# A hand-ordered attention and two-layer kernel: its order of steps rewritten, the last output bank cut into three pieces, all last stores issued from SyncE

## The chip, the cores and the metric

The kernel runs on one core of a Trainium2 chip. The metric is the time of one execution in device microseconds (us). Before the change it is 221.39 us, the median of three runs (221.13 to 222.2).

## The reference

There are 8 batches with 8 heads, 512 tokens and 32 states per head, and 64 numbers per vector. Per batch and head, attention runs both ways between tokens `x` and states `state`; per token the heads' results are put side by side, and the 8 x 544 rows of 512 go through two layers with a PReLU between them.

```python
scores  = scale * x @ state.T;  a  = softmax(scores);   xread = a  @ state   # 512 token rows
scores2 = scale * state @ x.T;  a2 = softmax(scores2);  sread = a2 @ x       # 32 state rows
x = concat([xread, sread]) -> rows of 512                                    # 4352 x 512
h = x @ w_in                                                                 # 512 -> 2048
g = max(h, 0) + alpha * min(h, 0)
out = g @ w_out                                                              # 2048 -> 512
```

## The kernel before

**The order is written out by hand.** `ORDER` (lines 17 to 101) is a list of some 1,050 tokens. Each names a step and its arguments (table `steps`, line 585), and the loop at line 599 issues them one after another. Nothing else orders the work: each engine runs its own instructions in the order of the tokens and waits for data and free buffers. So a token that is moved is moved past others only on the engines and queues that it uses. Batches are called groups below: 0 to 7 are the token rows of the batches, group 8 stands for the state rows of all batches.

**What the tokens are.** In `S.2.3.6` the numbers are the group, the block of 128 token rows and the pair of inner blocks; a further number is the PSUM bank (0 to 5), which is named when a tile is opened. A letter a, v or p says whether ScalarE, VectorE or GpSimd does a step.

- *Loads, all from GpSimd's queue:* `lx0.g` (half of the first group's x, line 177), `lst` (states, 190), `wi.f` (a quarter of w_in, 196), `wo.i` (a quarter of w_out, 202), `lx.b` (x of group b, 161; buffer of 4). `id` builds the identity for transposes on GpSimd, between loads.
- *Transposes:* `xt`/`xo` turn x of groups 0 and 1 on TensorE and copy it out (276, 281); `xd.b` does it by DMA from SyncE's queue for the later groups (268). `stc`, `stt`, `sto`, `str`, `sro` do the states (236, 230, 244, 258). `Z` issues products of zeros (215).
- *Scores:* `sc.b` (290; `sc.0.0` and `sc.0.1` are halves of group 0) writes the tile "two", which spans two banks. For the token direction follow `sb` (VectorE transposes 32x32 blocks, 323), `smax` (331), `ssh` (subtract, 337), `sexp` (343), `ssum` (347, 348), `snorm` (351) and `wb` (transpose back, 359). For the state direction `tm` (371), `te` (382), `tsum` (392), `tn` (GpSimd multiplies by 1/sum, 396), `tt` (DMA transpose from SyncE's queue, 400), `rd` (state reads on TensorE, 415) and `rdo` (copy out, 426).
- *The first layer is folded into the states:* `m.b.f` multiplies the states of group b with a quarter f of w_in (440, products of 64*32), in two halves: into two banks when banks are named, otherwise into tile "two". `mo` casts each half to SBUF (462).
- *First layer:* `F.b.jc` multiplies those by the attention weights (473; for group 8 it is w_in by the state reads, 482); `f` is one half of it (494). `N` makes relu(-h) on ScalarE (505) and `G` the PReLU on VectorE (513).
- *Second layer:* `S.b.q.j` adds two of 16 products into one bank (525); `R` is the same for group 8 (570). `O` and `RO` copy a finished bank to SBUF and store it from SyncE's queue (562, 563, 580, 582).
- *The last bank* (group 7, block 3) is cut in two halves of 256 columns, in banks of their own: `L.7.3.i` (542) and `LO.7.3.i` (553, 554). A store by `LO` goes out from ScalarE's queue if ScalarE made the copy, else from SyncE's.

A bank is taken again only when its last reader is done: a product that opens a bank can wait for a copy on ScalarE or VectorE, and all products behind it on TensorE wait too.

Of the kernel before, what the change touches and what calls it, by code (L numbers as in the profile page):

```python
# [8 lines left out]
F32 = mybir.dt.float32  # L9
# [8 lines left out]
lx0.0 stc id lx0.1 Z.1.22 stt.0 lst Z.2.20 xt.0.0.0.1 xo.0.0.0.a sto.v xt.0.1.0.2 oma xo.0.1.0.v  # L18
Z.0.4 xt.0.0.1.3 sc.0.0 sb.0.0 smax.0.0 xt.0.1.1.4 xo.0.0.1.a xo.0.1.1.a Z.0.3 str.1.5 sc.0.1 wi.0
lx.1 str.0.0 wi.1 ssh.p.0.0 sb.0.1 smax.0.1 Z.1.3 sc.0 sro.1.a Z.5.7 m.0.0.1.2 sro.0.a ssh.p.0.1  # L20
sexp.0.0 mo.0.0.a.1 tm.0 m.3.0.3.4 sexp.0.1 ssum.0.0 mo.0.0.a.0 mo.3.0.a.0 wo.0 snorm.p.0.0 te.0.0
ssum.0.1 snorm.p.0.1 m.1.0.5.0 Z.2.8 m.2.0.2.1 xt.1.0.0.3 mo.2.0.a.0 xt.1.1.1.2 mo.1.0.a.0 wi.2 wo.1
mo.1.0.v.1 wb.0.0 xt.1.0.1.0 xo.1.0.0.v wb.0.1 xt.1.1.0.5 xo.1.1.1.v mo.3.0.a.1 te.0.1 f.0.0.0.3
mo.2.0.a.1 xo.1.0.1.v f.0.0.1 tsum.0 N.0.0 xo.1.1.0.v m.1.1.4.2 m.0.1 mo.0.1.v.0 f.0.1.0.0
mo.0.1.a.1 f.0.1.1 wi.3 F.0.3.1 tn.0.1 F.0.7.5 mo.1.1.v.0 N.0.1 f.0.2.0.4 mo.1.1.a.1 f.0.2.1 F.0.5.2
wo.2 G.0.0 N.0.3 G.0.1 N.0.2 N.0.7 tn.0.0 G.0.3 N.0.5 lx.2 G.0.2 m.4.0 F.0.4.3 mo.4.0.a.1 S.0.0.0.0
G.0.7 S.0.1.0.1 S.0.0.1 S.0.1.1 N.0.4 m.0.2.4.5 G.0.5 mo.4.0.a.0 sc.1 S.0.2.0.2 G.0.4 mo.0.2.a.0
m.1.2.3.4 wo.3 mo.0.2.a.1 mo.1.2.a.1 S.0.2.1 F.0.6.5 mo.1.2.a.0 sb.1 tm.1 N.0.6 F.0.9.4 F.0.10.3
S.0.0.2 S.0.2.2 G.0.6 N.0.9 smax.1 te.1.1 S.0.1.2 te.1.0 F.0.11.5 N.0.11 S.0.1.3 S.0.2.3 G.0.9 m.0.3
# [5 lines left out]
S.0.0.7 O.0.0.a tm.2 F.1.5.2 lx.3 S.0.3.6 G.1.3 N.1.5 F.1.9.1 G.1.5 tn.1.0 xd.3 te.2.0 F.1.1.0 N.1.1
F.1.4.4 S.0.3.7 te.2.1 F.1.7.2 G.1.6 rd.0.3 N.1.4 O.0.3.a m.2.3 G.1.1 tt.1 F.1.8.0 F.1.10.5 smax.2
rdo.0.a mo.2.3.a.0 S.1.1.0.3 S.1.1.1 N.1.7 G.1.4 N.1.9 S.1.1.2 F.1.11.4 N.1.10 G.1.7 S.1.2.0.2
S.1.1.3 G.1.9 S.1.2.1 ssh.p.2 F.1.13.1 G.1.10 F.1.12.5 N.1.8 G.1.8 N.1.11 sexp.2 N.1.13 S.1.1.4
N.1.12 F.1.15.0 G.1.11 ssum.2 S.1.2.2 G.1.12 N.1.15 F.1.14.4 S.1.2.3 S.1.1.5 N.1.14 S.1.2.4 S.1.2.5
mo.2.3.a.1 G.1.13 G.1.15 m.2.1.5.1 m.3.2 S.1.2.6 G.1.14 snorm.p.2 mo.3.2.v.1 S.1.1.6 mo.3.2.a.0  # L40
# [12 lines left out]
S.2.3.4 S.2.3.5 S.2.3.6 G.3.4 m.4.1.3.2 G.3.14 te.4.1 m.4.3.1.0 ssh.p.4 m.5.1 sexp.4 G.3.2
mo.4.1.v.1 mo.4.1.v.0 mo.4.3.a.0 mo.4.3.v.1 ssum.4 rd.3.5 rd.2.2 F.3.0.1 mo.5.1.a.1 S.2.2.0.3
rdo.2.a F.3.11.0 lx.6 snorm.p.4 N.3.0 F.3.3.2 mo.5.1.a.0 S.2.2.1 N.3.11 S.2.2.2 G.3.0 S.2.2.3
S.2.3.7 F.3.10.1 G.3.11 N.3.3 G.3.3 rdo.3.a wb.4 m.4.2.5.0 tsum.4 mo.4.2.a.1 sc.5 F.3.5.2 S.2.2.4
S.2.2.5 tm.5 F.4.2.0 S.2.2.6 mo.4.2.a.0 N.3.10 tn.4.0 N.3.5 S.3.1.0.5 G.3.5 S.2.2.7 S.3.1.1 F.4.7.2
N.4.2 O.2.3.a tn.4.1 te.5.0 S.3.0.0.4 G.3.10 O.2.2.a N.4.7 G.4.2 F.3.12.1 G.4.7 F.4.6.0 S.3.1.2
# [46 lines left out]
def kernel(  # L105
# [526 lines left out]
```

## Time and profile before

| | |
|---|---|
| median of 3 runs | 221.39 us |
| profiled execution | 221.47 us |
| its span, first to last instruction | 219.7 us |
| TensorE products | 210.4 us busy, 1667 instructions |
| VectorE / ScalarE / GpSimd | 166.0 / 137.3 / 71.1 us busy |
| DMA moved | 23.12 MB, 8.62 of them from GpSimd's queue |
| granted TensorE clock | 1.000 of full speed |

All times in the profile count from the first instruction of the span. A row of the timeline gives the start, how long the group of instructions lasted, the engine (PE is TensorE's products, PEld its weight loads, DVE VectorE, ACT ScalarE, POOL GpSimd, SP SyncE), the line, the operation, output and input tiles, the shape, the count, and in brackets how long the engine had been idle and who ended that. Products overlap: one starts while the one before still drains, so the difference of two starts tells what a group costs. A row of a group of instructions gives the busy total, the mean of one in ns, and the idle time before them. A row of the DMA issues gives the KB of each and the us from issue to landing.

### The profile page before, as it was taken

What the parts mean: (1) busy time and instruction counts of PE and PEld (TensorE: products, weight loads), DVE (VectorE), ACT (ScalarE), POOL (GpSimd) and SP (SyncE); (2) the same over time, 40 slices, a digit from 0 to 9 for tenths busy, and PEclk for the clock granted to TensorE, in tenths of its full rate; (3) what the DMA queues carried; (4) which work ended last, traced back from release to release, by engine and by line L of the source; (5) the groups of instructions that cost most, each with busy time, mean ns of one, the idle gap of its engine ahead of it and who ended that gap; (6) DMA issues with size and microseconds to landing.
All of it is one profiled execution on the core that took longest, in us unless ns stands there. A gap on an engine that the chain in (4) does not pass through costs nothing.

```text
span 219.7 us, 4233 instructions
## 1 busy us (share of the span) xinstructions
PE 210.4 (96%) x1667; PEld 102.0 (46%) x1667; DVE 166.0 (76%) x251; ACT 137.3 (63%) x269; POOL 71.1 (32%) x58
## 2 busy tenths in 40 slices
PE   8678999999999999999999999999999999999992
PEld 7442334444344444544444444444446555644451
DVE  1499989899899989998867998598778775762022
ACT  2598974698699756977573987573665474631010
POOL 7289333452323493371713254003530000000000
PEclk9999999999999999999999999999999999999999
DMA  7999999998891176758930217110132011101034
GB/s 71 184 196 182 187 201 159 157 151 171 100 221 48 51 95 160 149 82 152 230 98 0 95 48 177 52 64 0 48 97 98 0 48 52 48 0 48 3 143 143
DMA packets 41028, 23.12 MB, mean 105 GB/s; under 512 B 24112, under 2 KB 36784, under 8 KB 41008
## 3 DMA queue, kind: packets, MB, share of 16 engines
q0 software_dynamic: 12704, 8.62, 28.2%
q1 hardware_dynamic: 26096, 14.09, 25.5%
q10 hardware_dynamic: 2208, 0.14, 0.7%
q8 instruction: 13, 0.21, 0.4%
q14 instruction: 7, 0.06, 0.1%
HBM read 17.31 MB, written 8.91 MB: 119 GB/s over the span
## 4 chain that ended last, share of the span: by engine, by line
PE 83%; DMA 8%; ACT 2%; POOL 2%; DVE 2%; issue 1%; POOLq 0%; ACTq 0%
PE o L525 45%; PE h L473 24%; DMA w_in_sb<-in_moe_w_in_dram 5%; PE m_ps L440 3%; PE h L482 3%; PE o L570 3%; DMA xT<-xg 3%; PE sr_ps L415 2%; PE o L542 2%; ACT neg L505 1%; DVE m L462 1%; ACT m L462 1%; POOL xg L177 1%; PE sc L290 1%; DVE gt L513 1%
## 5 line engine op out<-in xcount | busy, mean ns | idle before, releaser
L525 PE MATMUL o<-w_out_sb,gt 128*128 128x512 f16 x496 | 124.4, 379 | 0.1
L505 ACT ACTIVATE neg<-h 128x512 f32<-128x512 f32 (+1 forms) x144 | 78.6, 583 | 45.6 <-PE h L473 34.9
L513 DVE SCALAR_TENSOR_TENSOR gt<-neg,oma_sb,h 128x512 f16<-128x512 f32 x128 | 89.5, 738 | 15.0 <-ACT neg L505 14.3
L525 PEld LDWEIGHTS <-gt 128*128 128x128 f16 x496 | 47.8, 98 | 56.5 <-issue 2.1
L473 PE MATMUL h<-aT,m 128*128 128x512 f16 x250 | 69.6, 380 | 0.5 <-ACT m L462 0.4
L473 PEld LDWEIGHTS <-m 128*128 128x128 f16 x250 | 23.6, 98 | 29.9 <-issue 3.5
L462 ACT CAST m<-m_ps 128x512 f16<-128x512 f32 x49 | 28.0, 603 | 7.9 <-PE m_ps L440 4.0
L396 POOL TENSOR_SCALAR e<-e,r 128x512 f16<-128x512 f16 x16 | 25.0, 1566 | 19.3 <-DVE r L392 13.4
L337 POOL TENSOR_TENSOR ts<-ts,mx 128x1024 f32<-128x1024 f32 (+1 forms) x9 | 15.5, 1718 | 45.8 <-DVE mx L331 45.8
L351 POOL TENSOR_TENSOR an<-ts,r 128x1024 f16<-128x1024 f32 (+1 forms) x9 | 15.4, 1718 | 22.6 <-DVE r L348 14.1
L562 ACT COPY osb<-o 128x512 f32<-128x512 f32 x22 | 12.7, 591 | 12.3 <-PE o L525 12.3
L562 DVE COPY osb<-o 128x512 f32<-128x512 f32 x9 | 6.2, 687 | 14.7 <-PE o L525 14.7
L382 ACT ACTIVATE e<-sc,nb 128x512 f16<-128x512 f32 x16 | 11.0, 698 | 1.7 <-DVE nb L374 1.7
L440 PE MATMUL m_ps<-w_in_sb,stT 64*32 64x512 f16 x256 | 11.7, 383 | 0.2 <-DMA w_in_sb<-in_moe_w_in_dram 0.2
L513 DVE SCALAR_TENSOR_TENSOR gs<-neg,oma_sb,h 128x256 f16<-128x256 f32 x16 | 7.3, 478 | 5.6 <-ACT neg L505 5.6
L462 DVE CAST m<-m_ps 128x512 f16<-128x512 f32 x15 | 9.7, 677 | 1.2 <-PE m_ps L440 1.0
L347 DVE TENSOR_REDUCE r<-ts 128x32 f32<-128x1024 f32 (+1 forms) x9 | 9.8, 1090 | 1.0 <-ACT ts L343 0.9
L359 DVE STREAM_TRANSPOSE aT<-an 128x1024 f16<-128x1024 f16 (+1 forms) x9 | 10.1, 1120 | 0.5 <-POOL an L351 0.5
L331 DVE TENSOR_REDUCE mx<-ts 128x32 f32<-128x1024 f32 (+1 forms) x9 | 9.8, 1091 | 0.1
L371 DVE TENSOR_REDUCE nb<-sc 128x2 f32<-128x1024 f32 x8 | 9.6, 1198 | 0.0
L323 DVE STREAM_TRANSPOSE ts<-sc 128x1024 f32<-128x1024 f32 x7 | 8.7, 1240 | 0.6 <-PE sc L290 0.6
L570 PE MATMUL o<-w_out_sb,gs 128*128 128x512 f16 x32 | 9.0, 379 | 0.0
(48 smaller groups left out, 116.7 us busy)
## 6 DMA issues: line engine op xcount, KB each, us to landing
out_dram<-osb SPq DMA_DIRECT2D x31, 256.0 KB, 2.3
xg<-in_x_dram POOLq DMA_DIRECT2D x7, 512.0 KB, 7.3
w_in_sb<-in_moe_w_in_dram POOLq DMA_DIRECT2D x4, 512.0 KB, 9.6
w_out_sb<-in_moe_w_out_dram POOLq DMA_DIRECT2D x4, 512.0 KB, 10.7
xg<-in_x_dram POOLq DMA_DIRECT2D x2, 256.0 KB, 4.9
out_dram<-osr SPq DMA_DIRECT2D x2, 256.0 KB, 2.5
st<-in_state_dram POOLq DMA_DIRECT2D x1, 224.0 KB, 5.8
e2T<-e SPq DMA_TRANSPOSE x8, 3.4
```

What stands on the lines that cost most here:

```text
L337: engine(e).tensor_tensor(ts, ts, over_blocks(cols(live["mx", b], j, S // N)), ALU.subtract)
L351: engine(e).tensor_tensor(blocks(cols(live["an", b], j, S)), blocks(cols(live["ts", b], j, S)), over_blocks(cols(live["r1", b], j, S // N) ...
L382: nc.scalar.activation(live["e2", b][:, g, :, :], live["sc", b][:, :, :, g, :].rearrange("p r j s -> p (r j) s"), EXP, bias=live["nb", b][ ...
L396: nc.gpsimd.tensor_scalar_mul(e2, e2, live["r2", b][:, g : g + 1])
L440: nc.tensor.matmul(t[N * k : N * (k + 1), :], st_head(b, h)[64 * r : 64 * r + 64, :], w_in_sb[64 * r : 64 * r + 64, c, 512 * f : 512 * (f ...
L462: copier(e)(m_tile(b)[:, f, g, :], live["mp", b, f][g])
L473: nc.tensor.matmul(h.rearrange("p (r j s) -> p r j s", r=2, j=2), ms[b][:, f, g, 128 * j : 128 * (j + 1)], weights(b, g), start=(g == 0), ...
L505: nc.scalar.activation(neg, h, RELU, bias=0.0, scale=-1.0)
L513: nc.vector.scalar_tensor_tensor(gt, negs.pop((b, jc)), oma_sb[:, jc : jc + 1], h, ALU.mult, ALU.add)
L525: nc.tensor.matmul(outs[b, q], gts[b, jc][:, 128 * q : 128 * (q + 1)], w_out_sb[:, jc, :], start=(jc == 0), stop=(jc == n_jc - 1),)
L562: copier(e)(osb, t)
L570: nc.tensor.matmul(outs[B, q], gts[B, jc][:, 128 * q : 128 * (q + 1)], w_out_sb[:, jc, :], start=(jc == 0), stop=(jc == n_jc - 1),)
```

## The change

1. `ORDER` is replaced as a whole. The same products are there, with these differences in what is issued: `id` comes after both `lx0`; `sc.0.0` comes ahead of `xt.0.1.1` and `xt.0.0.1`; `m.0.1` and others get banks of their own or tile "two"; small products (`m`, `sc`, `rd`) are gathered into fewer stretches, one of them of eight; `tt.0` stands ahead of `xd.2`, and `rd.0` right behind `sc.2`; `lx.4` stands ahead of `lx.3`; `ssh.5`, `snorm.5` and `snorm.7` go from GpSimd to VectorE; several copies change between ScalarE and VectorE; 64 products of zeros instead of 67.
2. The last bank is cut into pieces of 256, 128 and 128 columns instead of two of 256.
3. All stores of `LO` are issued from SyncE.
4. The outputs of group 2 (`O.2.q`) are stored as two halves of 256 columns each.

```diff
 ORDER = """
-lx0.0 stc id lx0.1 Z.1.22 stt.0 lst Z.2.20 xt.0.0.0.1 xo.0.0.0.a sto.v xt.0.1.0.2 oma xo.0.1.0.v
-Z.0.4 xt.0.0.1.3 sc.0.0 sb.0.0 smax.0.0 xt.0.1.1.4 xo.0.0.1.a xo.0.1.1.a Z.0.3 str.1.5 sc.0.1 wi.0
...
-F.0.8.4 G.0.11 mo.0.3.v.0 S.0.0.3 S.0.3.0.5 N.0.10 ssh.p.1 xd.2 mo.0.3.a.1 S.0.3.1 N.0.8 sexp.1
...
-S.1.2.7 mo.2.1.a.1 mo.2.1.a.0 S.1.1.7 O.1.2.a O.1.1.a m.3.1.0.4 sc.3 m.2.2.1.5 lx.4 S.1.0.0.2 wb.2
...
-L.7.3.1.3 L.7.3.1.4 L.7.3.0.5 O.7.0.a L.7.3.0.6 L.7.3.1.5 O.6.3.a O.7.1.v L.7.3.1.6 RO.0.v L.7.3.0.7
-LO.7.3.0.v L.7.3.1.7 LO.7.3.1.a
+stc lx0.0 lx0.1 oma id Z.1.20 stt.0 Z.2.18 xt.0.0.0.1 sto.a xt.0.1.0.2 xo.0.0.0.v lst xo.0.1.0.v
+Z.0.6 sc.0.0 xt.0.1.1.3 xt.0.0.1.4 sb.0.0 xo.0.0.1.v smax.0.0 xo.0.1.1.a str.0.5 sc.0.1 str.1.0 wi.0
...
+F.0.13.0 sexp.1 tn.0.1 S.0.2.4 N.0.13 S.0.3.3 ssum.1 G.0.13 S.0.0.4 F.0.14.3 tn.0.0 S.0.2.5 tt.0
+S.0.1.4 N.0.14 G.0.14 F.0.12.0 m.1.3 S.0.3.4 snorm.p.1 F.0.15.3 xd.2 S.0.3.5 wb.1 N.0.12 S.0.1.5
...
+mo.2.1.a.0 m.3.2 S.1.1.3 F.1.10.3 F.1.13.0 mo.2.1.a.1 S.1.1.4 N.1.10 F.1.15.1 ssum.2 G.1.10 S.1.2.3
+N.1.13 N.1.14 N.1.15 S.1.2.4 G.1.13 S.1.1.5 mo.3.2.a.1 G.1.14 S.1.2.5 S.1.2.6 mo.3.2.a.0 sc.3
+m.3.1.3.0 G.1.15 m.2.2.2.1 snorm.p.2 S.1.2.7 wb.2 S.1.1.6 mo.3.1.a.1 mo.3.1.a.0 S.1.1.7 tt.1
...
+O.2.0.a S.2.3.7 G.3.7 O.2.1.v m.6.0 m.5.0.2.4 m.4.2.1.5 G.3.1 O.2.3.a mo.6.0.a.1 rd.2.3 mo.6.0.v.0
+mo.4.2.a.0 rd.3.0 snorm.p.4 mo.5.0.a.1 mo.4.2.v.1 m.4.1.1.5 sc.5 rdo.2.v rdo.3.v lx.6 mo.5.0.a.0
+mo.4.1.a.0 m.5.1.3.4 mo.4.1.a.1 mo.5.1.a.0 F.3.10.0 S.2.2.0.2 F.3.11.1 F.3.5.5 N.3.10 S.2.2.1
...
+LO.7.3.1.v R.1.7 L.7.3.2.1 RO.1.v L.7.3.0.6 L.7.3.0.7 S.7.1.7 L.7.3.2.2 LO.7.3.0.v O.7.1.a L.7.3.2.3
+L.7.3.2.4 L.7.3.2.5 L.7.3.2.6 L.7.3.2.7 LO.7.3.2.a
 """

-    def second_half(b, q, i, jc2, k=None):
-        w = d_model // 2
+    pieces = ((0, 256), (256, 384), (384, 512))
+
+    def second_piece(b, q, i, jc2, k=None):
+        lo, hi = pieces[i]
+        w = hi - lo
...
-                w_out_sb[:, jc, w * i : w * (i + 1)],
+                w_out_sb[:, jc, lo:hi],
...
-    def second_half_out(b, q, i, e):
-        w = d_model // 2
-        osb = moe.tile([128, w], F32, name=f"osb_{b}_{q}_{i}", tag="osr", bufs=2)
+    def second_piece_out(b, q, i, e):
+        lo, hi = pieces[i]
+        osb = moe.tile([128, hi - lo], F32, name=f"osb_{b}_{q}_{i}", tag=f"osr{i}", bufs=1)
         copier(e)(osb, outs.pop((b, q, i)))
-        (nc.scalar if e == "a" else nc.sync).dma_start(
-            token_rows(b, q)[:, w * i : w * (i + 1)], osb
-        )
+        nc.sync.dma_start(token_rows(b, q)[:, lo:hi], osb)

     def second_out(b, q, e):
...
         copier(e)(osb, t)
-        nc.sync.dma_start(rows, osb)
+        w = 256 if b == 2 else 512
+        for c in range(0, d_model, w):
+            nc.sync.dma_start(rows[:, c : c + w], osb[:, c : c + w])
```

More of the change, by code (lines that the diff above doesn't have):

```diff
@@ L35 @@
[L35 to L40, printed above, removed]
@@ L53 @@
[L53 to L58, printed above, removed]
@@ new lines @@
+Z.0.6 sc.0.0 xt.0.1.1.3 xt.0.0.1.4 sb.0.0 xo.0.0.1.v smax.0.0 xo.0.1.1.a str.0.5 sc.0.1 str.1.0 wi.0
+sro.0.a lx.1 wi.1 ssh.p.0.0 sb.0.1 Z.1.3 sc.0 Z.5.7 m.0.0.1.2 sro.1.a sexp.0.0 smax.0.1 m.3.0.3.4
+ssh.p.0.1 tm.0 mo.0.0.a.1 sexp.0.1 ssum.0.0 m.1.0.5.0 ssum.0.1 te.0.1 te.0.0 mo.1.0.v.1 wo.0
+mo.1.0.a.0 snorm.p.0.0 mo.3.0.a.1 Z.2.10 xt.1.1.1.2 xt.1.1.0.5 mo.0.0.a.0 snorm.p.0.1 wb.0.0
+mo.3.0.a.0 m.2.0 xt.1.0.1.0 xo.1.1.0.v xt.1.0.0.4 f.0.0.0.1 f.0.1.0.5 wi.2 mo.2.0.a.0 wb.0.1
+mo.2.0.a.1 f.0.1.1 xo.1.0.0.v N.0.1 m.0.1.3.4 f.0.0.1 mo.0.1.a.1 m.1.1 xo.1.1.1.v N.0.0 xo.1.0.1.v
```

134 lines of the change are left out of this document (68 added, 66 removed).

## The prediction

> **What bounds the kernel now.** I read the page first (busy times, then the span in 40 slices), then the timeline of TensorE from end to end, because almost nothing else can matter when one engine is busy this much.
>
> ```profile
> PE 210.4 (96%) x1667; PEld 102.0 (46%) x1667; DVE 166.0 (76%) x251; ACT 137.3 (63%) x269; POOL 71.1 (32%) x58
> ...
> PE   8678999999999999999999999999999999999992
> ```
>
> TensorE is full from the fifth slice to the last but one. So time can be won in four places only: the first 27 us, what TensorE spends on changing between shapes, the few waits left in the middle, and the end after its last product. The profiled execution took 221.47 us, of which the span is 219.7; the median of the runs is 221.39, 0.08 less. The sum is made against 221.47.
>
> The PE rows give the price of a product and of a change of shape:
>
> ```profile
> L525 PE MATMUL o<-w_out_sb,gt 128*128 128x512 f16 x496 | 124.4, 379 | 0.1
> ```
> ```profile
> 88.55 0.84 PE L440 MATMUL m_ps<-w_in_sb,stT 64*32 64x512 f16 x24
> 89.32 1.19 PE L415 MATMUL sr_ps<-e2T,xg 128*64 128x32 f16 x64
> 90.44 0.61 PE L473 MATMUL h<-aT,m 128*128 128x512 f16 x2
> ...
> 108.38 1.03 PE L525 MATMUL o<-w_out_sb,gt 128*128 128x512 f16 x4
> 109.34 0.68 PE L415 MATMUL sr_ps<-e2T,xg 128*64 128x32 f16 x32
> 109.95 0.63 PE L440 MATMUL m_ps<-w_in_sb,stT 64*32 64x512 f16 x16
> 110.51 0.61 PE L473 MATMUL h<-aT,m 128*128 128x512 f16 x2
> ```
>
> One product lasts 0.379, four last 1.03, so they start (1.03 - 0.379) / 3 = 0.217 apart. Four should free TensorE after 0.87, but the state reads (L415) begin 0.96 after the first: 0.09 for the change. One set of state reads takes 0.61 and two take 90.44 - 89.32 = 1.12, so a set is 0.51 and leaving it costs 0.10. Three tokens m (L440) take 0.77 and two take 0.56: 0.21 each, and 0.13 to leave. I take **0.11 per change** between the three kinds: whole products, state reads (128*64), and m or scores (64*32).
>
> **The change, part by part.** The order is rewritten as a whole, so I split it at S.0.0.2, the first product that needs the second quarter of w_out. In both orders the same 13 tokens of whole products (F and S) and the same m and scores stand before it.
>
> *The head.*
>
> ```profile
> 8.23 0.40 PE L276 MATMUL xT_ps<-ident,xg 128*128 128x128 f16 x4 [1.80 <-DMA xg<-in_x_dram]
> ...
> 26.91 0.38 PE L525 MATMUL o<-w_out_sb,gt 128*128 128x512 f16 x1
> ```
> ```profile
> 9.93 2.08 ACT L258 COPY stT<-st_ps 128x896 f16<-128x896 f16 x2
> ...
> 18.91 0.58 ACT L462 CAST m<-m_ps 128x512 f16<-128x512 f32 x1 [0.66 <-DVE m L462]
> ```
> ```profile
> 2.19 0.23 POOL masks.py:197 MEMSET ident<- 128x128 f16 x1
> ...
> 2.73 0.78 POOL L177 DMA_DIRECT2D xg<-in_x_dram  x1
> ...
> 16.88 0.75 POOL L202 DMA_DIRECT2D w_out_sb<-in_moe_w_out_dram  x1
> ```
> ```profile
> w_out_sb<-in_moe_w_out_dram POOLq DMA_DIRECT2D x1, 512.0 KB, 9.7
> ```
> ```profile
> 5.00:6.00 1.00, 1.00 (x20) 0.97 (x19) 0.00 (x0) 0.00 (x0) 1.00 (x2) 1.00 1.13 120
> 6.00:7.00 1.00, 0.43 (x8) 0.26 (x5) 0.42 (x1) 0.58 (x1) 0.44 (x1) 1.00 1.44 192
> ```
>
> Today sc.0.0 stands behind the transposes that wait 1.80 for the second half of x; it would now run in that gap. But its exp (sexp.0.0) comes after both copies sro on ScalarE, which end at 12.01 either way, so I give this nothing by itself. More useful: two f products move ahead of the wait for w_in's second quarter, and m.0.1 gets two banks of its own. Today its cast on ScalarE waits 0.66 for VectorE's cast of the other half of tile "two". S.0.0.2 can therefore be reached sooner; but its weights land at 16.88 + 9.7 = 26.6, and it runs at 26.91. **The head wins at most 0.31**, unless the loads come sooner: -0.31 (from +0.3, if nothing is won and the two more changes of shape ahead of this point cost 0.2, to -0.31).
>
> The loads may come a little sooner, since the second half of x is issued ahead of the identity, 2.73 - 2.19 = 0.54 earlier. The last two rows show 120 GB/s between 5 and 6 us and 192 after it; filling that dip is worth 1 - 120/192 = 0.38 us of the stream that every weight stands in. I take half: **-0.2** (0 to -0.38). All POOL loads keep their order up to there.
>
> *Changes of shape.* From S.0.0.2 on, the old order has 39 and the new one 32 (fewer, longer stretches, up to eight small products in one): 7 x 0.11 = **-0.77** (0.09 to 0.13 each: -0.6 to -0.9).
>
> *A wait that goes.*
>
> ```profile
> 58.36 0.41 PE L440 MATMUL m_ps<-w_in_sb,stT 64*32 64x512 f16 x8
> ...
> 58.80 0.60 PE L440 MATMUL m_ps<-w_in_sb,stT 64*32 64x512 f16 x8
> 59.50 0.59 PE L525 MATMUL o<-w_out_sb,gt 128*128 128x512 f16 x2
> ```
>
> The last m should free TensorE after 0.21 + 0.13 = 0.34, at 59.14, but S.1.0.0 starts at 59.50: it takes bank 2 and m.2.2 takes banks 1 and 5, just filled by others and not yet copied out. The new order puts other banks there: **-0.36** (0 if something else is late).
>
> *A wait that comes.* The stretch of eight is m.6.0, m.5.0, m.4.2, rd.2, rd.3, m.4.1, sc.5, m.5.1, and m.4.1 wants banks 1 and 5, which m.4.2 filled a moment before.
>
> ```profile
> ACT m L462 <- DVE m L462: 3.6, 3, 2.0
> ```
> ```profile
> L462 ACT CAST m<-m_ps 128x512 f16<-128x512 f32 x49 | 28.0, 603 | 7.9 <-PE m_ps L440 4.0 <-DVE m L462 3.6
> L562 ACT COPY osb<-o 128x512 f32<-128x512 f32 x22 | 12.7, 591 | 12.3 <-PE o L525 12.3
> ```
> ```profile
> L462 DVE CAST m<-m_ps 128x512 f16<-128x512 f32 x15 | 9.7, 677 | 1.2 <-PE m_ps L440 1.0
> ```
>
> Bank 5 is emptied by VectorE after its cast of m.6.0, and that one waits for ScalarE's cast of the other half (the three waits in the first row are of this kind), which stands behind the store copy O.2.3. Counted from the start of m.6.0: copy 0.1 to 0.69, cast to 1.29, VectorE's casts to 1.97 and 2.65; engines overlap successive instructions by about 0.1, so 2.5 or so. TensorE comes to m.4.1's second half after 0.77 + 1.12 + 0.1 = 2.0. **+0.6** (0 to 0.75). Behind it wait sc.5, m.5.1 and all the products.
>
> *The transposes of x for group 2.* On SyncE, xd.2 now stands behind tt.0.
>
> ```profile
> 34.35 2.44 SPq L268 DMA_TRANSPOSE xT<-xg  x1
> 36.84 1.63 SPq L400 DMA_TRANSPOSE e2T<-e  x1
> ```
> ```profile
> 41.08 0.41 PE L290 MATMUL sc<-xT,stT 64*32 64x256 f16 x16 [0.17 <-DMA xT<-xg]
> ```
> ```profile
> DMA to landing us min/median/max: 3.7/4.6/8.6
> ```
> ```profile
> 28.89 1.91 POOL L337 TENSOR_TENSOR ts<-ts,mx 128x1024 f32<-128x1024 f32 x1 [4.89 <-DVE mx L331]
> ```
> ```profile
> L396 POOL TENSOR_SCALAR e<-e,r 128x512 f16<-128x512 f16 x16 | 25.0, 1566 | 19.3 <-DVE r L392 13.4 <-issue 5.8
> ```
>
> sc.2 already waits 0.17 for xd.2, which took 6.69 from its issue. tt.0 needs two multiplies of 1.57 on GpSimd, which stood ahead of ssh.p.1 and are now behind it: 28.89 + 1.91 + 3.13 = 33.9, or up to 0.5 sooner with the head. Its own issue takes 1.63, so xd.2 starts at 35.0 to 35.6 instead of 34.35, and sc.2 comes at about the same time as today. If the data move no faster, the wait grows by all of that; if the loads that share the DMA engines end meanwhile, by less; if tt.0's data go first and fully, by more. **+0.4** (-0.17 to +1.3). rd.0, next to sc.2 now, needs tt.0, which is ahead.
>
> *The last bank and the stores.*
>
> ```profile
> 15.68 0.87 PE L276 MATMUL xT_ps<-ident,xg 128*128 128x128 f16 x12 [0.17 <-ACT m L462]
> 16.39 0.38 PE L494 MATMUL h<-aT,m 128*128 128x512 f16 x1
> ...
> 213.56 2.13 PE L542 MATMUL o<-w_out_sb,gt 128*128 128x256 f16 x18
> ```
> ```profile
> 215.72 0.37 ACT L553 COPY osb<-o 128x256 f32<-128x256 f32 x1 [3.70 <-PE o L542]
> ```
> ```profile
> out_dram<-osb SPq DMA_DIRECT2D x1, 128.0 KB, 2.0
> out_dram<-osb ACTq DMA_DIRECT2D x1, 128.0 KB, 2.3
> ```
>
> Products 256 wide start 0.11 apart (18 in 2.13, the last of them seen in full); those 128 wide (12 transposes with a weight load each) (16.39 - 15.68) / 12 = 0.059. 32 narrow ones replace 16: 32 x 0.059 - 16 x 0.11 = **+0.13**. The ends: 0, since half the width can't take less than half the time, and 32 x 0.098 - 1.76 = +1.4, if each takes as long as its weight load:
>
> ```profile
> L525 PEld LDWEIGHTS <-gt 128*128 128x128 f16 x496 | 47.8, 98 | 56.5 <-issue 2.1
> ```
>
> The transposes have such loads too and are not held up by them, so I stay near the low end. The Trainium skill, TensorE: Matmul & The Clock Gate, section Back-to-back issue gap, speaks against narrow products: a stream of weight loads and products is said to need about 81 ns each at 128 columns. By that figure this term would be +0.83 and the forecast 221.5. The trace disagrees, with 59 ns.
>
> The last copy is shorter (0.37 at 256 wide), but ScalarE first copies O.7.1 (0.59), only six narrow products before the end; and the store lands in 2.0 instead of 2.3: **-0.1** (-0.4 to +0.4).
>
> *At nothing:* group 2's outputs stored as two halves (four more issues on SyncE, hidden by its idle time; tt.4 behind them has its reader far away); three zero products fewer (TensorE idles there); ssh.5, snorm.5 and snorm.7 from GpSimd to VectorE, three instructions of 128x1024 on an engine 76% busy, some 1.35 each (twice the cast above; below GpSimd's 1.91). Their cover is the products in other banks; where it is gone, a prelu behind them is late and TensorE waits for its bank, 1.35 each at worst.
>
> Sum: -0.31 - 0.2 - 0.77 - 0.36 + 0.6 + 0.4 + 0.13 - 0.1 = -0.61; 221.47 - 0.61 = 220.86, and **220.8** against the median.
>
> **Rivals.** *Both new waits stay away and the loads gain fully:* -0.31 - 0.38 - 0.77 - 0.36 + 0.13 - 0.1 = -1.79, **219.6**. For it: SyncE and GpSimd idle most of the time. Against it: the same-tile wait is in the table of waits. *Slower: xd.2 behind tt.0.* Without my +0.4 the sum is -1.01. If xd.2 takes the longest landing on record, 8.6, from an issue at 35.3, sc.2 runs at 43.9 instead of 41.08: +2.8, **223.2**. It decides from a wait of 2.1 us on. For it: it is issued while loads still come; against it: its median is 4.6. *The long stretches give back what they save:* casts pile up behind the stretches of five, four and three as behind the eight, and the 0.77 is gone: **221.6**. *Narrow products bound by their weight loads:* +1.4 instead of +0.13, **222.1**. The Trainium skill's 81 ns, above, lies between.
>
> **How the numbers follow.** Forecast 0.46 (its own range 220.0 to 221.7), faster rival 0.26, slower rival 0.14, stretches 0.10, narrow products 0.04. A measurement of this kernel tells about 0.5% (1.1 us) from no change. Faster: the first rival and the low edge of the forecast, 0.30; slower: the second rival and a little of the last two, 0.15; within: 0.55. Range 219.5 to 222.6: it holds the first rival and part of the second.
>
> **What would show it.** Right: S.0.0.2 waits for w_out at about 26.5; m.4.1 waits 0.6 on a VectorE cast near 90; sc.2 waits under 1 us on xT; no wait at the place of 59.50; narrow L-pieces 0.06 apart. Wrong: any wait of over 1 us in the middle, or TensorE at S.0.0.2 later than 26.9.

## The result and the profile after

The changed kernel took 220.48 us (median of 22 runs, 219.44 to 221.76), the kernel before beside it 221.95 (22 runs). The ratio is 0.9937, interval 0.9917 to 0.9957, so 1.4 us (0.95 to 1.84) off 221.39, where 0.6 was forecast: the right side and inside the range, but the forecast was a little under half of the size. The profiled execution took 219.44, the shortest of the 22; its span is 217.7, 2.0 below that of before.

The page of the changed kernel, busy times and TensorE's slices:

```profile
span 217.7 us, 4268 instructions
...
PE 209.6 (96%) x1680; PEld 103.1 (47%) x1680; DVE 169.5 (78%) x256; ACT 135.6 (62%) x268; POOL 65.2 (30%) x55
...
PE   7879999999999999999999999999999999999993
```

TensorE still bounds everything. So the two timelines of TensorE can be laid side by side token by token: the 2.0 splits into 0.95 up to the product S.0.0.2 (26.91 to 25.96), 0.78 from there to the start of the last product (188.50 to 187.72), and 0.26 behind it (4.26 to 4.00). Where the old order reached w_in's second quarter:

```profile
17.49 0.63 PE L440 MATMUL m_ps<-w_in_sb,stT 64*32 64x512 f16 x16 [0.19 <-DMA w_in_sb<-in_moe_w_in_dram]
```

The head of the new order on TensorE's timeline, from the product of zeros in the gap to S.0.0.2:

```profile
12.44 0.72 PE L216 MATMUL z<-zero 128*128 128x128 f16 x10 [0.33 <-ACT m L463]
14.07 0.40 PE L277 MATMUL xT_ps<-ident,xg 128*128 128x128 f16 x4 [0.91 <-DMA xg<-in_x_dram]
...
15.89 0.81 PE L495 MATMUL h<-aT,m 128*128 128x512 f16 x3
17.06 0.41 PE L441 MATMUL m_ps<-w_in_sb,stT 64*32 64x512 f16 x8 [0.36 <-DMA w_in_sb<-in_moe_w_in_dram]
17.40 0.39 PE L495 MATMUL h<-aT,m 128*128 128x512 f16 x1
...
25.96 1.89 PE L526 MATMUL o<-w_out_sb,gt 128*128 128x512 f16 x8
```

Three first products (15.89) now run ahead of the wait for w_in's second quarter, which ends at 17.06. From there S.0.0.2 is 8.90 away, where the old order took 26.91 - 17.49 = 9.42. Behind S.0.0.2 the wait forecast for m.4.1 is there. In the stretch of eight, m.4.1's two halves are 0.66 apart:

```profile
87.93 0.84 PE L441 MATMUL m_ps<-w_in_sb,stT 64*32 64x512 f16 x24
88.70 1.19 PE L416 MATMUL sr_ps<-e2T,xg 128*64 128x32 f16 x64
89.82 0.40 PE L441 MATMUL m_ps<-w_in_sb,stT 64*32 64x512 f16 x4
90.48 0.40 PE L441 MATMUL m_ps<-w_in_sb,stT 64*32 64x512 f16 x4 [0.27 <-DVE m L463]
```

The releaser is VectorE, as forecast; its own casts in the same stretch waited 1.06 for ScalarE's first half of m.6.0:

```profile
89.14 1.29 DVE L463 CAST m<-m_ps 128x512 f16<-128x512 f32 x2 [1.06 <-ACT m L463]
```

(The 0.27 counts from the modelled end of a product; the stretch as a whole is 0.68 longer than its products and changes of shape.) The products 128 wide of the last bank start 0.056 apart: the row of twelve lasts 0.83, the last of them seen in full (0.22). The row of six holds two of them and four of the piece that is 256 wide: 2 x 0.056 + 4 x 0.109 = 0.55, which is when the next whole product starts. Behind them SyncE's stores queue up:

```profile
212.08 0.71 PE L546 MATMUL o<-w_out_sb,gt 128*128 128x128 f16 x6
212.63 0.59 PE L526 MATMUL o<-w_out_sb,gt 128*128 128x512 f16 x2
...
213.00 0.55 SPq L586 DMA_DIRECT2D out_dram<-osr  x1
213.06 0.83 PE L546 MATMUL o<-w_out_sb,gt 128*128 128x128 f16 x12
...
213.64 0.54 SPq L558 DMA_DIRECT2D out_dram<-osb  x1
213.93 0.27 ACT L557 COPY osb<-o 128x128 f32<-128x128 f32 x1
214.28 0.40 SPq L567 DMA_DIRECT2D out_dram<-osb  x1
214.77 0.41 SPq L558 DMA_DIRECT2D out_dram<-osb  x1
```

The last piece is copied at 214.20 and its store is issued at 214.77: it stands 0.57 behind three others.

### The profile page after: what moved, and what is told of

Same layout as the page of the kernel before. It is cut to its first block, busy times and chain, and to the rows that moved or that the text cites. A ratio compares the mean times of both kernels' runs of the same rounds, so it can differ in the third digit from the quotient of the medians.

```text
span 217.7 us, 4268 instructions
## 1 busy us (share of the span) xinstructions
PE 209.6 (96%) x1680; PEld 103.1 (47%) x1680; DVE 169.5 (78%) x256; ACT 135.6 (62%) x268; POOL 65.2 (30%) x55
## 4 chain that ended last, share of the span: by engine, by line
PE 87%; DMA 8%; POOL 2%; issue 1%; ACT 1%; DVE 1%; POOLq 0%
PE o L526 48%; PE h L474 24%; DMA w_in_sb<-in_moe_w_in_dram 5%; PE m_ps L441 3%; PE h L483 3%; PE o L574 3%; DMA xT<-xg 3%; PE o L546 2%; PE sr_ps L416 2%; PE sc L291 1%; DVE m L463 1%; POOL xg L178 1%; POOL xg L162 0%; PE h L495 0%; POOL w_in_sb L197 0%
## 5 line engine op out<-in xcount | busy, mean ns | idle before, releaser
L506 ACT ACTIVATE neg<-h 128x512 f32<-128x512 f32 (+1 forms) x144 | 77.2, 580 | 46.8 <-PE h L474 36.3
L474 PE MATMUL h<-aT,m 128*128 128x512 f16 x250 | 68.2, 379 | 0.0
L338 POOL TENSOR_TENSOR ts<-ts,mx 128x1024 f32<-128x1024 f32 (+1 forms) x8 | 13.6, 1697 | 33.6 <-DVE mx L332 33.6
L564 ACT COPY osb<-o 128x512 f32<-128x512 f32 x20 | 11.7, 595 | 17.1 <-PE o L526 17.1
L352 POOL TENSOR_TENSOR an<-ts,r 128x1024 f16<-128x1024 f32 (+1 forms) x7 | 11.6, 1663 | 19.7 <-DVE r L349 14.3
L564 DVE COPY osb<-o 128x512 f32<-128x512 f32 x11 | 7.4, 686 | 6.8 <-PE o L526 6.8
L463 DVE CAST m<-m_ps 128x512 f16<-128x512 f32 x12 | 8.1, 685 | 2.7 <-ACT m L463 1.9
L483 PE MATMUL h<-XS,w_in_sb 128*128 128x256 f16 x64 | 9.1, 273 | 0.0
L344 ACT ACTIVATE ts<-ts 128x1024 f32<-128x1024 f32 (+1 forms) x9 | 8.8, 974 | 0.0
```

The lines of the kernel that those rows point to most:

```text
L338: engine(e).tensor_tensor(ts, ts, over_blocks(cols(live["mx", b], j, S // N)), ALU.subtract)
L352: engine(e).tensor_tensor(blocks(cols(live["an", b], j, S)), blocks(cols(live["ts", b], j, S)), over_blocks(cols(live["r1", b], j, S // N) ...
L463: copier(e)(m_tile(b)[:, f, g, :], live["mp", b, f][g])
L474: nc.tensor.matmul(h.rearrange("p (r j s) -> p r j s", r=2, j=2), ms[b][:, f, g, 128 * j : 128 * (j + 1)], weights(b, g), start=(g == 0), ...
L483: nc.tensor.matmul(h, w_in_sb[:, c, 128 * jc : 128 * (jc + 1)], XS[:, c].rearrange("p q n b -> p (q n b)"), start=(c == 0), stop=(c == n_c ...
L506: nc.scalar.activation(neg, h, RELU, bias=0.0, scale=-1.0)
```

## Experiments

Each profile gives the same marks on TensorE's timeline. All are in us; the ratio is against the kernel before beside it. "w_in" is the start of the first product that needs w_in's second quarter; "to last" runs from S.0.0.2 to the start of the last product, "to end" from there to the end of the span in the trace. (The recorded expectations took "to end" from spans rounded to 0.1; so they say 4.02 and 3.65 where the table has 4.00 and 3.60.)

| kernel | ratio (interval) | w_in | S.0.0.2 | to last | to end |
|---|---|---|---|---|---|
| before | | 17.49 | 26.91 | 188.50 | 4.26 |
| changed | 0.9937 (0.9917-0.9957) | 17.06 | 25.96 | 187.72 | 4.00 |
| same_again | 0.9956 (0.9926-0.9986) | 17.44 | 26.33 | 188.01 | 3.98 |
| before_x_first | 0.9972 (0.9952-0.9991) | 17.49 | 26.91 | 188.26 | 4.25 |
| before_loads_first | 1.0013 (0.9991-1.0034) | 17.47 | 26.89 | 188.26 | 4.26 |
| after_loads_late | 0.9975 (0.9949-1.0002) | 16.95 | 25.84 | 188.51 | 3.97 |
| after_f_behind | 0.9963 (0.9937-0.9989) | 17.73 | 27.25 | 188.15 | 4.00 |
| after_copy_on_dve | 0.9944 (0.9921-0.9967) | 17.05 | 25.94 | 188.13 | 3.97 |
| after_xd_first | 0.9937 (0.9905-0.9969) | 17.21 | 26.10 | 187.52 | 3.99 |
| after_two_halves | 0.9927 (0.9896-0.9958) | 17.41 | 26.30 | 187.96 | 3.60 |
| after_casts_swapped | 0.9965 (0.9947-0.9983) | 17.72 | 27.27 | 188.31 | 3.97 |
| after_more_visits | 1.0035 (1.0005-1.0065) | 17.10 | 26.00 | 189.51 | 4.00 |
| after_more_zeros | 0.9959 (0.9944-0.9975) | 17.34 | 26.34 | 188.56 | 3.97 |
| combined | 0.9873 (0.9835-0.9911) | 17.23 | 26.12 | 187.19 | 3.99 |

The intervals are 0.4 to 0.8 us wide on each side, as much as most single edits are worth or more, so the verdicts rest on the marks. Each kernel has one profile, so its marks are those of one execution.

**Is the head luck?** The theory after the first two profiles was that the head had been won by loads that land earlier; the rival, that the new order of small products and copies won it.

> The changed kernel unchanged, once more. In its first profile TensorE came to S.0.0.2 at 25.96 us (26.92 before the change) and the span was 217.7, which is the shortest of its runs. If the 0.96 of the head belongs to the kernel, a second profile has S.0.0.2 at 25.8 to 26.2, 193 GB/s between 4 and 6 us and about 205 GB/s between 18 and 24.5. If it was luck of that one execution, S.0.0.2 comes 0.3 or more later. From S.0.0.2 to the last product both say 187.7 us, since no load is waited for there. Ratio 0.992 to 0.996.

S.0.0.2 came at 26.33: 0.58 earlier than before, not 0.95. The gain is the kernel's, and some 0.4 of the first profile was that execution's. The rates were nearly those of the first profile (190 GB/s between 4 and 6 us and 204 between 18 and 24.5, against 193 and 205), so they do not set S.0.0.2.

```diff
-lx0.0 stc id lx0.1 Z.1.22
+lx0.0 stc lx0.1 id Z.1.22
```

> The kernel before, with one token moved: the second half of x is issued ahead of the identity. Theory 'loads' (everything up to the state scores waits for the stream that starts with x, and the stream of before has a dip to 120 GB/s between 5 and 6 us): the dip goes, the states and w_in's first quarter land about 0.5 sooner, sc.0 moves from 11.04 to 10.4-10.6 and S.0.0.2 from 26.92 to 26.3-26.6; ratio about 0.998. Theory 'order' (the head was won by the new order of small products and copies): the dip may go, but S.0.0.2 stays at 26.8-27.0; ratio 1.000.

```diff
-... F.0.3.1 tn.0.1 F.0.7.5 ... wo.2 ... tn.0.0 ... lx.2 ... wo.3
+... F.0.3.1 F.0.7.5 ... wo.2 ... lx.2 ... wo.3 tn.0.1 tn.0.0
```

> The kernel before, with two tokens moved: GpSimd's two multiplies tn.0 stand behind the last quarter of w_out instead of between the loads. Theory 'loads': the rate between 18 and 24.5 us rises from 169 to about 200 GB/s, the last loads land 1 to 2 us sooner, S.0.0.2 stays (its own load came before it was needed), and the wait of sc.2 for x of group 2 (0.23) shrinks or goes, as SyncE's transposes meet fewer loads; ratio 0.998 to 0.999. Theory 'order' (the rate between 18 and 24.5 is luck or has another cause): the rate stays below 185 and sc.2 waits as before or, since tt.0 is later, longer; ratio 1.000 to 1.002.

The rates of both stretches, of before_loads_first (the last column is GB/s):

```profile
4.00:6.00 2.00, 2.00 (x22) 1.99 (x20) 0.37 (x2) 0.00 (x0) 2.00 (x4) 1.00 1.36 181
18.00:24.50 6.50, 6.12 (x61) 2.18 (x54) 6.07 (x10) 5.41 (x11) 5.55 (x6) 1.00 1.21 196
```

It has no dip at 5 us though its identity still stands ahead of x's second half, and before_x_first has 193 GB/s between 18 and 24.5 though its multiplies still stand between the loads. So both dips of the profile before were that execution's. In both kernels the loads are earlier (w_out's second quarter lands at 25.3 and 25.5, not 26.6) and S.0.0.2 stays at 26.9. For the head **the theory "loads" fell.** The two kernels have the same marks and ratios of 0.9972 and 1.0013. That before_x_first is a little faster than before, which the theory "order" did not expect, and why the two differ stays open (the lowered clock, below, was in one run of 12 of either). The rows of before_loads_first that show what holds S.0.0.2:

```profile
17.47 0.62 PE L440 MATMUL m_ps<-w_in_sb,stT 64*32 64x512 f16 x16 [0.27 <-ACT m L462]
...
19.53 0.39 PE L473 MATMUL h<-aT,m 128*128 128x512 f16 x1 [0.23 <-ACT m L462]
...
20.51 0.59 PE L473 MATMUL h<-aT,m 128*128 128x512 f16 x2 [0.15 <-ACT m L462]
...
26.89 1.46 PE L525 MATMUL o<-w_out_sb,gt 128*128 128x512 f16 x6
```

In the old order S.0.0.2 comes 9.42 after w_in's second quarter in all three profiles, and the waits inside are for ScalarE's casts. In before_loads_first what the first of these rows waits for last is a cast too, since the load landed at 17.42. In the new order it is 8.89 to 8.90 in every profile at full clock but one (9.00 with the zeros).

```diff
-... tsum.0 ... wo.2 ... lx.2 wo.3 ... tn.0.1 ... tn.0.0
+tsum.0 ... tn.0.1 wo.2 ... tn.0.0 lx.2 wo.3 ...
```

> The changed kernel with the two multiplies tn.0 put back between the loads on GpSimd, as they stood before. Theory 'loads': the rate between 18 and 24.5 falls to about 170 GB/s, wo.3 lands 1 to 2 us later, xd.2's data come later and sc.2 waits 0.5 to 1.5 instead of 0.20; S.0.0.2 stays within 0.3 of 25.96; the time is 0.5 to 1.5 us above that of the changed kernel. Theory 'order': rate and waits as in the changed kernel, no difference in time over 0.3 us.

S.0.0.2 stayed (25.84), but sc.2 waited 0.99 for x of group 2. The rate between 18 and 24.5 us did not fall to 170 GB/s as expected (197), but x of group 2, the load behind the second multiply, landed at 34.38 and not at 32.41. The later loads were not felt in the head; they were felt there.

```diff
-f.0.0.0.1 f.0.1.0.5 wi.2 ... f.0.1.1 xo.1.0.0.v N.0.1 m.0.1.3.4 f.0.0.1 mo.0.1.a.1
+f.0.0.0.1 wi.2 ... xo.1.0.0.v m.0.1.3.4 f.0.0.1 f.0.1.0.5 f.0.1.1 mo.0.1.a.1 N.0.1
```

> The changed kernel with the first products f.0.1.0 and f.0.1.1 put back behind m.0.1, which waits for w_in's second quarter (in the change they run in that wait). Theory 'order of the head': what the head won is the 8.89 us from the product that w_in's second quarter releases to S.0.0.2, against 9.42 before, in every trace so far; two products more behind the wait make it 9.3 to 9.4, and S.0.0.2 comes 0.4 to 0.5 later than it would. Rival 'landing': only the time at which w_in lands decides; the stretch stays at 8.9. Time: 0.4 us against 0 (under what the ratio can tell).

The clock was lowered in this execution up to 18.0 (below), so I count from f.0.0.1 on:

```profile
18.26 0.82 PE L495 MATMUL h<-aT,m 128*128 128x512 f16 x3
...
27.25 1.89 PE L526 MATMUL o<-w_out_sb,gt 128*128 128x512 f16 x8
```

8.99 against 25.96 - 17.40 = 8.56 in the changed kernel: 0.43, two products at 0.216. What runs in the wait for w_in is won in full.

**The transposes of x.**

```diff
-tt.0 S.0.1.4 N.0.14 G.0.14 F.0.12.0 m.1.3 S.0.3.4 snorm.p.1 F.0.15.3 xd.2
+xd.2 tt.0 S.0.1.4 N.0.14 G.0.14 F.0.12.0 m.1.3 S.0.3.4 snorm.p.1 F.0.15.3
```

> The changed kernel with the two DMA transposes on SyncE back in their old order, xd.2 ahead of tt.0. sc.2 waited 0.20, 0.41 and 0.99 in three traces of the new order and 0.23, 0 and 0 in three of the old one. Theory 'behind tt.0 costs': xd.2 starts 1 us or more earlier, sc.2 waits under 0.1, and rd.0 behind it may wait up to 0.5 for tt.0 instead. Rival 'free': both land when the loads let them, and sc.2 plus rd.0 wait 0.2 to 0.4 together as now.

SyncE and TensorE of after_xd_first:

```profile
32.88 2.49 SPq L269 DMA_TRANSPOSE xT<-xg  x1
35.42 1.30 SPq L401 DMA_TRANSPOSE e2T<-e  x1
```
```profile
38.79 1.46 PE L526 MATMUL o<-w_out_sb,gt 128*128 128x512 f16 x6
40.18 0.41 PE L291 MATMUL sc<-xT,stT 64*32 64x256 f16 x16
40.52 0.68 PE L416 MATMUL sr_ps<-e2T,xg 128*64 128x32 f16 x32
```

The same places in the changed kernel:

```profile
32.94 1.59 SPq L401 DMA_TRANSPOSE e2T<-e  x1
34.72 1.68 SPq L269 DMA_TRANSPOSE xT<-xg  x1
```
```profile
40.22 0.41 PE L291 MATMUL sc<-xT,stT 64*32 64x256 f16 x16
```

xd.2 starts at 32.9 instead of 34.7, sc.2 does not wait, nor does rd.0 behind it, and 187.52 is 0.20 less than 187.72. That is the wait of sc.2 in the first profile: a wait counts here from when the products before it should have freed TensorE, and a short one has no bracket in its row. In the other profiles with xd.2 behind tt.0 and the loads as in the change, that wait was 0.41, 0.62, 0.72, 0.52, 0.56, 0.66 and, once, 0. The mean of the eight is 0.46; the three of the old order had 0.23, 0 and 0.

**The wait of m.4.1.**

```diff
-O.2.3.a mo.6.0.a.1 rd.2.3 mo.6.0.v.0
+O.2.3.v mo.6.0.a.1 rd.2.3 mo.6.0.v.0
```

> The changed kernel with one copy (O.2.3, the store copy ahead of the casts of the stretch of eight small products) moved from ScalarE to VectorE. My theory of the 0.68 that m.4.1 waits there is the row of ScalarE's store copy, ScalarE's cast of one half of m.6.0, VectorE's cast of the other half, VectorE's cast of bank 5; without the first link the wait is 0.2 to 0.4, and everything behind comes 0.3 to 0.5 earlier. Rival: bank 1 or TensorE itself sets that wait, and it stays at 0.6 to 0.7; or VectorE, now longer busy, makes a prelu late and gives it back within 3 us.

The wait went from 0.68 to 0.56 only. Without the copy, ScalarE's cast waits for its product, which takes 0.48 from the start of the stretch to the start of the cast: the copy had been beside that. The next kernel takes VectorE's place in the chain instead.

```diff
-mo.6.0.v.0 mo.4.2.a.0 rd.3.0 snorm.p.4 mo.5.0.a.1 mo.4.2.v.1
+mo.4.2.v.1 mo.6.0.v.0 mo.4.2.a.0 rd.3.0 snorm.p.4 mo.5.0.a.1
```

> The changed kernel with two of VectorE's casts in the stretch of eight swapped: bank 5's (m.4.2) ahead of m.6.0's second half, which must wait for ScalarE's first half. Taking the store copy out of the chain had shortened the wait of m.4.1 only from 0.68 to 0.56, since the copy lay beside the 0.48 that m.6.0's products need. Theory now: what costs is VectorE waiting for the half of a shared tile with another cast queued behind; then m.4.1 waits at most 0.1 and sc.5, which reuses m.6.0's tile, 0.1 to 0.25: together 0.1 to 0.3 instead of 0.68, and everything behind comes 0.4 to 0.55 sooner. Rival: ScalarE's casts (bank 1 and m.5.0) are as late, and the sum stays over 0.5.

TensorE in after_casts_swapped:

```profile
90.17 0.84 PE L441 MATMUL m_ps<-w_in_sb,stT 64*32 64x512 f16 x24
90.95 1.19 PE L416 MATMUL sr_ps<-e2T,xg 128*64 128x32 f16 x64
92.06 0.41 PE L441 MATMUL m_ps<-w_in_sb,stT 64*32 64x512 f16 x8
92.46 0.41 PE L291 MATMUL sc<-xT,stT 64*32 64x256 f16 x16
```

The gap inside m.4.1 is gone and the stretch is 0.33 longer than its work: 0.35 won, a little less than the 0.4 to 0.55 expected. The cast queued behind a wait for the other half of a shared tile is half of the 0.68; the other half stays open.

**The price of a change of shape.**

```diff
-m.2.1.0.1 G.1.11 sexp.2 mo.2.1.a.0 m.3.2 S.1.1.3
+m.2.1.0.1 G.1.11 sexp.2 mo.2.1.a.0 S.1.1.3 m.3.2
-m.6.1.4.0 m.7.0 S.4.0.7
+m.6.1.4.0 S.4.0.7 m.7.0
```

(and m.2.2, rd.1 and m.7.2 in the same way)

> The changed kernel with five small sets (m.3.2, m.2.2, rd.1, m.7.0, m.7.2) each moved behind the next product or pair, which splits four stretches into two and one mixed one into two: 41 changes of shape from S.0.0.2 on instead of 32. Theory 'price per change': four visits more at 0.223 and one at 0.13, the last product comes 1.0 later with respect to S.0.0.2 (187.7 in the changed kernel), waits apart. Rival 'the long stretches give back': shorter stretches spare waits for casts, and less than 0.5 is lost.

From S.0.0.2 to the last product 189.51, 1.79 more. Of it 0.46 is a longer wait of sc.2 and 0.31 a wait in the visit of m.3.3; 1.02 is left, the sum expected. No wait became shorter. The rival, that long stretches give back, fell for the five stretches that were split; the stretch of eight was left whole, and its 0.68 is a wait of this kind.

**The last bank.**

```diff
-    pieces = ((0, 256), (256, 384), (384, 512))
+    pieces = ((0, 256), (256, 512))
-        nc.sync.dma_start(token_rows(b, q)[:, lo:hi], osb)
+        (nc.scalar if e == "a" else nc.sync).dma_start(token_rows(b, q)[:, lo:hi], osb)
```

> The changed kernel with its last bank in two halves again (the second half where the last piece stood, its store issued from ScalarE's queue, as before the change). Theory: narrow products are nearly free (32 at 0.0555 against 16 at 0.109: 0.03), and what the end won lies behind the last product: 3.95 to 4.02 us from there to the end of the span with three pieces, 4.22 to 4.26 with two; this kernel shows 4.2 to 4.3, and is 0.2 to 0.3 slower. Rival 'the last copy and SyncE's queue eat it': 4.0 or less, and no slower.

The theory was wrong: behind the last product it takes 3.60, less than with three pieces. The end of after_two_halves:

```profile
212.62 0.59 PE L526 MATMUL o<-w_out_sb,gt 128*128 128x512 f16 x2
...
214.56 0.37 ACT L557 COPY osb<-o 128x256 f32<-128x256 f32 x1 [0.72 <-PE o L546]
214.96 0.36 ACTq L558 DMA_DIRECT2D out_dram<-osb  x1
```

The copy ends at 214.93 and the store goes at once; with three pieces the store stood 0.57 behind others on SyncE. From S.0.0.2 to the end of the span, without the wait of sc.2, it is 187.96 + 3.60 - 0.52 = 191.04 against 187.72 + 4.00 - 0.20 = 191.52. Two halves are 0.48 better. The edit changes the pieces and the queue together; the last kernel below, with three pieces and the other queue, takes them apart.

**The clock.**

```diff
-Z.2.10 xt.1.1.1.2
+Z.2.30 xt.1.1.1.2
```

> The changed kernel with 30 products of zeros instead of 10 in the gap at 12.4 us, where TensorE waits for x of group 1. Theory 'clock': executions come in two kinds, about 1.1 us apart, with a mean granted clock of 1.00 and of 0.992; the profile of an execution of the second kind shows the clock at 0.50 from 14.4 to 18.0, right behind a gap of 1.67 without products. 15 of 33 runs of the changed kernel and 25 of 66 of the kernel before were of that kind. With the gap filled, at most 2 of 12 are, and the median falls by 0.3 to 0.6. Rival: what TensorE does in the gap does not matter, 4 to 7 of 12 stay so, or the zeros delay x's transposes and the time rises by up to 0.3.

The slices of the granted clock that led to this are those of after_f_behind (the number third from the right):

```profile
14.00:15.00 1.00, 0.19 (x3) 0.19 (x4) 1.00 (x3) 1.00 (x4) 1.00 (x2) 0.81 1.25 207
15.00:18.00 3.00, 3.00 (x33) 1.79 (x31) 1.85 (x5) 2.25 (x5) 3.00 (x5) 0.50 1.25 207
18.00:19.00 1.00, 1.00 (x11) 0.21 (x3) 1.00 (x3) 0.59 (x1) 1.00 (x2) 0.98 1.23 200
```

A share of 0.81 is 0.38 us at half clock, 0.98 is 0.04: the clock was at half from 14.62 to 18.04, for 3.4 us.

With the gap filled, no run of 12 had the lowered clock, against 58 of 110 of the changed kernel and its seven variants that keep the ten zeros (13 of 21 of the two measured beside it). That part of the theory holds. The gain in time of 0.3 to 0.6 did not show: 220.59 in the median. The profile has the zeros' price (8.89 became 9.00) and a new loss, which other profiles of this order have as well:

```profile
57.00 0.41 PE L291 MATMUL sc<-xT,stT 64*32 64x256 f16 x16 [0.96 <-DMA xT<-xg]
```
```profile
47.03 7.71 SPq L269 DMA_TRANSPOSE xT<-xg  x2
```

sc.3 waits for x of group 3, whose transpose now stands behind that of group 4 on SyncE: xd.4, then xd.3, take 7.71 to issue here, and 4.92 in the first profile of the changed kernel, where sc.3 did not wait. I had priced xd.2 and not this.

**All that the runs point to.**

```diff
-Z.2.10 ... tt.0 ... xd.2 ... lx.4 ... lx.3 ... xd.4 ... xd.3 ... mo.6.0.v.0 ... mo.4.2.v.1
+Z.2.30 ... xd.2 tt.0 ... lx.3 ... lx.4 ... xd.3 ... xd.4 ... mo.4.2.v.1 mo.6.0.v.0
-        nc.sync.dma_start(token_rows(b, q)[:, lo:hi], osb)
+        (nc.scalar if e == "a" else nc.sync).dma_start(token_rows(b, q)[:, lo:hi], osb)
```

> The changed kernel with five edits that the runs point to: xd.2 ahead of tt.0 (sc.2 waited 0.20 to 0.99 in seven traces and not with this edit), loads and DMA transposes of groups 3 and 4 in the order 3, 4 (sc.3 waited 0.07 to 1.03 in four of ten traces, behind xd.4 on SyncE), VectorE's two casts swapped (0.68 to 0.33), 30 zero products in the gap at 12.4 us (no run of 12 with the lowered clock, where about half had it), and the last piece's store issued from ScalarE (3.65 us from the last product to the end against 4.02). Theory, that these are separate and each holds: against the runs of the changed kernel at full clock (220.1 to 220.5) 0.2 to 0.6 for the transposes, 0.35 for the casts, 0.3 for the store, and no run at the lowered clock: median 219.0 to 219.6, ratio 0.988 to 0.992. Rival, that time won ahead is lost again to later waits or that the spread comes from elsewhere: median 220.0 or more, ratio 0.994 or more.

219.05 us, ratio 0.9873 (0.9835 to 0.9911): better than both kernels, and at the fast end of what was expected. No run of 6 had the lowered clock, sc.2 and sc.3 do not wait, and S.0.0.2 to the last product is 187.19, that is 187.72 less 0.20 and 0.35. The store gave nothing:

```profile
213.86 0.39 ACTq L558 DMA_DIRECT2D out_dram<-osb  x1
213.91 0.41 SPq L567 DMA_DIRECT2D out_dram<-osb  x1
```

With the last piece out of SyncE's queue (the first row, landed at 215.77), the 256 KB of O.7.1 (the second row, landed at 216.32) end last, and the end is 3.99. So the queue in front of the last store is not what the three pieces cost. What differs is when O.7.1 can be copied: its last product, S.7.1.7, starts 212.63 - 25.96 - 0.20 = 186.47 behind S.0.0.2 with three pieces and 212.62 - 26.30 - 0.52 = 185.80 with two halves (again without the wait of sc.2), because more of the last piece's products are left to run behind it.

## Why the prediction was right, and where it was not

By its own steps, measured on the two first profiles:

| step | forecast | measured |
|---|---|---|
| head | -0.31 | -0.53 (9.42 to 8.89) |
| loads | -0.2 | -0.43 (17.49 to 17.06) |
| changes of shape | -0.77 | -0.77 |
| wait before S.1.0.0 | -0.36 | -0.36 |
| wait of m.4.1 | +0.6 | +0.68 |
| xd.2 behind tt.0 | +0.4 | -0.04 |
| narrow products | +0.13 | +0.03 |
| behind the last product | -0.1 | -0.26 |
| not named | 0 | -0.36 |

- **Changes of shape and the two waits** came out to within 0.1, and after_more_visits repeats the price by adding changes. Single visits cost 0.223 beyond their products, a third change in a visit some 0.09. The chain given for m.4.1 was right only in part, though: without its first link, the store copy, 0.56 of the wait is left, and VectorE's queued cast makes half of it.
- **The head** was mis-sized by its bound. "S.0.0.2 waits for w_out at 26.6" came from one execution; in two others of the old order that quarter landed at 25.3 and 25.5, and S.0.0.2 still came at 26.9. The sign named for it, a wait for w_out at about 26.5, did not come: in the changed kernel the quarter landed at 24.73, ahead of S.0.0.2 at 25.96. What held it was the chain behind w_in's second quarter, which the same profile showed as waits for ScalarE's casts. In the new order one first product fewer stands behind that landing and two of these waits are gone: 0.53. My "three zero products fewer cost nothing" left out that products of zeros can matter for the clock (last section); whether those three did is not shown.
- **Loads**: w_in's second quarter was needed at 17.47 to 17.49 in three profiles of the old order and at 16.95 to 17.44 in the nine full-clock profiles of the new one (mean 17.20). That is 0.2 to 0.3; the first profile's 0.43 was a good draw. But the cause named, the dip at 5 us, is not it: the two variants of the old order have no dip, and w_in's second quarter lands there at 17.45 and 17.42, with the dip at 17.45. What brings it sooner in the new order stays open.
- **xd.2 behind tt.0** looks like a miss on the first pair of profiles. Over all of them sc.2 waits 0.46 in the new order and 0.08 in the old, so +0.4 was the size, and undoing this part takes the wait away. The slower rival needed 2.1 us of wait; the longest seen was 0.99, with late loads.
- **The last bank** had the wrong sign in one part. The 0.26 won behind the last product come from the order of the last products and stores, which with two halves wins 0.66 there (4.26 to 3.60). The three pieces, forecast at +0.13 - 0.1 against two halves, cost 0.48. I priced a shorter copy and a faster landing, and not that O.7.1's copy and store would end the program.
- **Not named**: a gap of 0.28 between two first products at 32.11 went, and 0.08 in two more. I had read the waits, and this one has none; what makes it stays open. TensorE before:

```profile
32.11 1.31 PE L473 MATMUL h<-aT,m 128*128 128x512 f16 x4
33.26 1.03 PE L525 MATMUL o<-w_out_sb,gt 128*128 128x512 f16 x4
```

Four products last 1.31 in the first row, where four in the second last 1.03.

Of the 2.0 between the first two profiles, 0.6 or so was the luck of the second: 0.15 of the loads (0.43 against 0.28 on the mean), 0.42 of sc.2. Runs whose mean granted clock stays above 0.992 have medians of 221.39 before (72 runs) and 220.19 changed (18): 1.20. The part left over against the forecast of 0.6 is the head, the gap at 32.11 and the end. The first profile's 219.44 is close to the faster rival's 219.6, but not for its reason: that rival had both new waits stay away, and m.4.1 waited 0.68.

## What to carry to other kernels

A bound that is a landing time needs more than one execution, or a look at what else ends at that point: here the same product came at 26.9 with its weights 1.3 earlier. Work that fits in a wait is won at its full price (0.43 for two products), and a change of shape costs the same 0.1 wherever it stands, so fewer visits pay as long as the casts behind them are ordered by what is needed next. A short last piece did not help here, even with its store alone on its queue: a larger store issued beside it ended last.

## What the runs showed of the hardware

**A gap of under 2 us can halve TensorE's clock for 3.4 us.** In two profiles the granted clock fell to 0.50 for 3.4 us, from 14.6 and, in after_casts_swapped, from 16.3 (0.63 in the slice from 16 to 17, 0.50 to 19, 0.66 to 20), after TensorE had waited 1.7 to 1.8 us for x of group 1. after_loads_late had the same wait, 1.7, and kept 1.00. In both drops the traces' record of the clock changes in steps of 3.41 us: it first reads full speed at 4.38 and 6.03, falls three steps later (14.62, 16.27) and rises one step behind that. TensorE was busy for 1.60 and 1.61 us (47%) of the step ahead of the drop, which held the whole wait; in after_loads_late a step ends inside the wait, and the busy time of the two is 57% and 84%. So where the steps fall seems to decide. It is not shown to be the rule: in the profile of before a step with 1.61 us busy (5.01 to 8.42) was not followed by a drop. The runs with the lowered clock (mean 0.992 or less) have medians 1.1 above the others: 222.48 and 221.39 before, 221.26 and 220.19 changed. They were 31 of 103 before, 15 of 33 of the changed kernel and 58 of 110 with its variants that keep the ten zeros. Beside each other, the kernel before had them in 9 of 35 runs, 16 of 31 and 3 of 26, the new order with ten zeros in 10 of 23, 25 of 44 and 13 of 21: more often each time, though hardly so the second. That m.2.0 stood in the gap and now stands behind it may be why; only the filled gap was tried. The Trainium skill, TensorE: Matmul & The Clock Gate, section Part 1: The HAM clock gate (the "warmup" mystery), says that the clock drops to half after about one idle window of 3.4 us, and that this window runs freely and does not start anew with a kernel. The 3.4 us of the drop, the steps and the drop's coming and going agree with that; the gap here was half of such a window.

**Narrow products are not bound by their weight loads here**: 0.0555 from start to start at 128 columns, each with a load of its own, 0.109 at 256, 0.216 at 512. The rival with the weight loads is out. So, for this stream, are the 81 ns of the Trainium skill, TensorE: Matmul & The Clock Gate, section Back-to-back issue gap.
